# Weight decoding with a mask on VectorE and 16-bit words from ScalarE, and a first key chunk in two halves

## The chip, the core and the metric

The kernel runs on one core of a Trainium2 chip. The metric is the device time of one execution in microseconds; three runs of the kernel before took 966.6, 967.17 and 967.68 us, median 967.17. In the text PE is TensorE, DVE VectorE, ACT ScalarE, POOL GpSimd, and SP SyncE, whose queue issues most DMAs.

## The reference

Attention by random features, then a layer norm and a two-layer MLP with a residual. With q, k, v of 8 batches x 8 heads x 576 rows x 64, 128 features, d_model 512 and 2048 hidden units:

```python
def phi(x):
    proj = np.einsum('bhsd,md->bhsm', x, omega)
    sq = np.sum(x * x, axis=-1, keepdims=True) / 2.0
    h = proj - sq
    h = h - np.max(h, axis=-1, keepdims=True)
    return np.exp(h) / np.sqrt(m)
q_p, k_p = (phi(q_s), phi(k_s))
kv = np.einsum('bhsm,bhsd->bhmd', k_p, v)
z = np.sum(k_p, axis=2)
num = np.einsum('bhsm,bhmd->bhsd', q_p, kv)
den = np.einsum('bhsm,bhm->bhs', q_p, z)[..., None] + 1e-06
...
xn = (x - mu) / np.sqrt(var + 1e-06) * g_ln
ch = np.maximum(xn @ w_ch1, 0.0) @ w_ch2
return (x + ch).astype(np.float32)
```

Everything is float32 at the interface; the weights `w_ch1` and `w_ch2` arrive as float64 and are passed to the chip as pairs of 32-bit words.

## The kernel before

The 4608 rows (8 batches x 576) are cut into 36 chunks of 128 rows (`NC`), four chunks to a token tile of 512 (`T`), nine tiles (`NT`). The hidden layer is cut into 16 blocks of 128 (`NF`), called f below; `f` of `mm1` makes one block of 128 hidden units for a whole tile, `f` of `mm2` adds that block's share to the four output banks.

**Attention.** `gen_k` (lines 600 to 635) treats one key chunk: load, product with omega on PE into a pair of PSUM banks (L621, 16 matmuls), maximum on DVE (L624), eight exponentials on ACT (L630). `gen_sums` (L637) multiplies the result with v (L665) and copies the sum to `kv`. `gen_q` (L746) treats a query chunk: load, product (L767, or L784/L785 from tile 2 on), copy to SBUF, maximum over partitions on POOL (L796), subtraction on DVE (L801), exponential on ACT (L804). One chunk of the first tile, number 3, takes its maximum over PE instead (`gen_q_pe`). `gen_x` (L827) multiplies both (L850), divides (L857 to L861) and hands the rows to `gen_xnT` (L923), which normalises (L934/L936) and transposes them, the first tile through PE (L979, L983, L985), the others through a transposing DMA (`gen_flip`, L947 to L970).

**Weights.** `gen_w` (L501 to L557) loads one weight tile, `[128, 512]` float64 as two 32-bit words `r[:, :, 0]` (low) and `r[:, :, 1]` (high), and makes of it two float32r tiles, a leading part and a rest. The sign bit and the top three bits of the low word are put together with the scaled high word shifted by three. There are two ways. If the planner gives the first step to ACT, the low word is scaled there (L515) and DVE joins it with the sign bit (L517); if to DVE, DVE masks the sign (L523) and shifts and joins the low word (L527). Both then scale the high word on ACT (L360) or DVE (L362) and join all on DVE (L531); then come the factor g for some of them (L539), the leading part and the rest (L549/L555). There are 32 tiles, all made while the first token tile is in the MLP or before.

**MLP.** `mm1` (L1009 to L1011) and `mm2` (L1050 to L1052) each take three float32r matmuls in place of one full-precision one: 24 per hidden block, 12 each. `relu` (L1023 on ACT, L1025 on DVE) stands between them.

**The order.** All work is written as generators that `yield` their next need: an engine and an estimated duration, a tile, a bank, an event. The class `Plan` is a list scheduler that runs while the program is built: it keeps a clock for each engine, takes the work that can start first and, among equals, the lowest rank, and so writes each engine's fixed instruction order. `rank` is given at `plan.add`; a table `SHIFT` adds an offset to the ranks of named generators, for instance `('gen_x', 1): -42` for chunk 1 (L115, L1144). A token tile is worth 32 ranks, one hidden block two. A part that may run on ACT or DVE says so by `either(a, d)` with a duration for each.

Attention work that needs banks while the MLP runs is a *visit* (L420): it is let in between two MLP blocks in the bank pair 0 and 1. With two visits waiting, the MLP's own pair 2 and 3 is lent as well and both go in one interruption (`serve`, L189). Before the MLP starts there are three bank pairs for visits (`pairs_now`, L427), and small matmuls on a tile `spin` (`gen_warm`, L1083) fill PE's idle time.

Of the kernel before, what the change touches and what calls it, by code (L numbers as in the profile page):

```python
# [15 lines left out]
U32 = mybir.dt.uint32  # L16
U16 = mybir.dt.uint16
AF = mybir.ActivationFunctionType
# [5 lines left out]
P = 128  # L24
# [284 lines left out]
def favor_ffn(ctx, tc, kT, kTr, vF, vR, qT, qD, omT, gT, w1, w2, out):  # L309
# [21 lines left out]
    def f32(ap):  # L331
        return ap.bitcast(F32)
# [7 lines left out]
    def dve2(n):  # L340
        return "run", {DVE: 0.07 + 0.00104 * n}, "two"

    def either(a, d):
        return "run", {ACT: a, DVE: d}, "two"
# [156 lines left out]
    def gen_w(n, f):  # L501
# [8 lines left out]
        wt = yield "get", n_big  # L510
        eng = yield either(0.58, 0.34)
        t = tile_of(wt, [P, DM], U32)
        sign = 0x80000000
        if eng == ACT:
            nc.scalar.activation(out=t, in_=r[:, :, 0], func=AF.Copy, scale=2.0**-29 * 7.49 / 8)  # L515
            yield dve2(DM)
            nc.vector.scalar_tensor_tensor(  # L517
                out=r[:, :, 0], in0=r[:, :, 1], scalar=sign, in1=t, op0=ALU.bitwise_and, op1=ALU.bitwise_or
            )
            eng = yield either(0.58, 0.34)  # L520
            scaled(eng, f32(r[:, :, 1]), f32(r[:, :, 1]), 2.0**-112)
        else:
            nc.vector.tensor_scalar(out=t, in0=r[:, :, 1], scalar1=sign, scalar2=None, op0=ALU.bitwise_and)  # L523
            eng = yield either(0.58, 0.34)
            scaled(eng, f32(r[:, :, 1]), f32(r[:, :, 1]), 2.0**-112)
            yield dve2(DM)
            nc.vector.scalar_tensor_tensor(  # L527
                out=r[:, :, 0], in0=r[:, :, 0], scalar=29, in1=t, op0=ALU.logical_shift_right, op1=ALU.bitwise_or
            )
        yield dve2(DM)  # L530
        nc.vector.scalar_tensor_tensor(  # L531
            out=t, in0=r[:, :, 1], scalar=3, in1=r[:, :, 0], op0=ALU.logical_shift_left, op1=ALU.bitwise_or
# [67 lines left out]
    def gen_k(b, c, kraw, early, owners, t_v, n_kp, last):  # L600
# [4 lines left out]
        nc.sync.dma_start(kraw, kT[b, c] if c < NFULL else kTr[b // 2])  # L605
# [9 lines left out]

        t_b = yield from visit("row", 0.95)
# [18 lines left out]
        done(("kp", b, c))  # L635

# [109 lines left out]
    def gen_q(c):  # L746
# [3 lines left out]
        if c < QF:  # L750
            qraw = tile_of(t_q, [P, 4 * P])
            yield dma(P * 4 * P)
            if c == 0:
                nc.scalar.dma_start(qraw, qT[c].rearrange("p a b -> p (a b)"))
                nc.scalar.preload_act_table_set("natural_log_exp_and_others")
            else:
                nc.sync.dma_start(qraw, qT[c].rearrange("p a b -> p (a b)"))
# [446 lines left out]
```

## Time and profile before

| | us |
|---|---|
| median of three runs | 967.17 |
| the profiled execution | 966.85 |
| its span, first to last instruction | 965.0 |
| first matmul of the MLP (L1009) starts | 33.94 |
| busy: PE, DVE, ACT, POOL | 956.5, 446.1, 412.4, 118.3 |

The page gives each engine's busy time over the span; the windows give it by stage; the timeline lists instructions by start, length, engine, line, tiles written and read, and in brackets an idle time of the engine ahead of it with what ended it. `ACTq` and `SPq` rows are DMA issues. Rows of groups end with the total busy time, the mean in ns, and the idle time before them. A matmul's length in the rows is more than its distance to the next, since matmuls overlap in the array; distances between starts tell what one costs.

### The profile page before, as it was taken

To read this page: it belongs to the slowest core of one execution; us is meant where nothing else is said; L and a number is where in the kernel's file an instruction comes from. 1 tells how busy PE (TensorE), PEld (TensorE's weight loads), DVE (VectorE), ACT (ScalarE), POOL (GpSimd) and SP (SyncE) were. 2 spreads that over 40 slices of the span, in tenths; PEclk is the share of its full clock that TensorE was granted. 3 is DMA by queue.
4 is the path that set the end of the run, shared out by engine and by line. 5 is a ranking of instruction groups with operands and counts; after the bars stand their busy time and mean duration, and the time that the engine had idled before them with its cause. 6 is when DMAs were issued, how large, how long until landed. Compare 5 with 4: busy or idle time off the path is not lost.

```text
span 965.0 us, 15968 instructions
## 1 busy us (share of the span) xinstructions
PE 956.5 (99%) x6732; PEld 786.3 (81%) x6732; DVE 446.1 (46%) x779; ACT 412.4 (43%) x759; POOL 118.3 (12%) x47
## 2 busy tenths in 40 slices
PE   9999999999999999999999999999999999999998
PEld 6877788888888888888878888888888888888886
DVE  7999976434435445335635346561542131113112
ACT  7898855444245454345355435450332121011010
POOL 5003103104001120020303013320110000000000
PEclk9999999999999999999999999999999999999999
DMA  8765461352143324115233223240212030002001
GB/s 299 240 242 198 165 186 67 89 143 66 66 100 110 122 77 138 50 45 175 59 107 103 74 96 91 88 153 1 87 45 77 1 99 1 1 1 87 1 1 44
DMA packets 70584, 91.45 MB, mean 95 GB/s; under 512 B 38000, under 2 KB 38384, under 8 KB 70512
## 3 DMA queue, kind: packets, MB, share of 16 engines
q1 hardware_dynamic: 70368, 90.17, 29.2%
q8 instruction: 53, 0.87, 0.4%
q10 hardware_dynamic: 144, 0.26, 0.1%
q14 instruction: 19, 0.16, 0.1%
HBM read 63.15 MB, written 18.87 MB: 85 GB/s over the span
## 4 chain that ended last, share of the span: by engine, by line
PE 91%; DVE 3%; ACT 3%; DMA 2%; issue 1%; DVEq 0%; SPq 0%; ACTq 0%
PE b L1050 13%; PE b L1009 13%; PE b L1011 13%; PE b L1010 13%; PE b L1052 13%; PE b L1051 13%; PE b L665 4%; PE b L850 3%; PE b L621 3%; PE b L785 1%; PE b L784 1%; DMA wide<-wide 1%; DMA quad<-qD 1%; PE b L767 1%; DVE w L517 0%
## 5 line engine op out<-in xcount | busy, mean ns | idle before, releaser
L1025 DVE SCALAR_TENSOR_TENSOR hid<-b,hid 128x512 fp32r<-128x512 f32 x144 | 99.2, 690 | 340.4 <-ACT hid L1023 339.9
L1050 PE MATMUL b<-w,hid 128*128 128x512 f32 x577 | 228.9, 397 | 0.0
L1009 PE MATMUL b<-xnT,w 128*128 128x512 f32 (+1 forms) x584 | 227.3, 389 | 1.4 <-ACT kp L630 1.4
L1052 PE MATMUL b<-w,hid 128*128 128x512 f32 x577 | 225.2, 390 | 0.6 <-DVE hid L1025 0.5
L1011 PE MATMUL b<-xnT,w 128*128 128x512 f32 (+1 forms) x584 | 225.7, 386 | 0.0
L1010 PE MATMUL b<-xnT,w 128*128 128x512 f32 (+1 forms) x584 | 225.6, 386 | 0.0
L1051 PE MATMUL b<-w,hid 128*128 128x512 f32 x577 | 224.8, 390 | 0.0
L1023 ACT ACTIVATE hid<-b 128x512 fp32r<-128x512 f32 x144 | 85.8, 596 | 294.2 <-PE b L1011 293.9
L796 POOL PARTITION_ALL_REDUCE quad<-quad x34 | 112.1, 3321 | 596.9 <-ACT quad L354 423.9
L1009 PEld LDWEIGHTS b<-xnT,w 128*128 128x128 f32 x584 | 109.7, 188 | 27.1 <-ACT kp L630 2.5
L1052 PEld LDWEIGHTS b<-w,hid 128*128 128x128 f32 x577 | 108.3, 188 | 25.4 <-DVE hid L1025 2.5
L1050 PEld LDWEIGHTS b<-w,hid 128*128 128x128 f32 x577 | 108.3, 188 | 24.6
L1011 PEld LDWEIGHTS b<-xnT,w 128*128 128x128 f32 x584 | 109.7, 188 | 22.4
L1010 PEld LDWEIGHTS b<-xnT,w 128*128 128x128 f32 x584 | 109.7, 188 | 21.7
L1051 PEld LDWEIGHTS b<-w,hid 128*128 128x128 f32 x577 | 108.4, 188 | 21.4
L630 ACT ACTIVATE kp<-b,mb 128x128 f32<-128x128 f32 x264 | 71.9, 393 | 37.3 <-DVE mb L624 36.6
L934 ACT ACTIVATE wide<-x,st 128x512 f32<-128x512 f32 x29 | 20.9, 722 | 80.5 <-DVE x L861 69.6
L624 DVE TENSOR_REDUCE mb<-b 128x8 f32<-128x1024 f32 x36 | 42.9, 1218 | 26.4 <-PE b L621 26.2
L801 DVE TENSOR_TENSOR quad<-quad,quad 128x1024 f32<-128x1024 f32 x34 | 51.3, 1512 | 8.1 <-POOL quad L796 7.9
L779 DVE TENSOR_TENSOR quad<-quad,quad 64x1024 fp32r<-64x1024 f32 x28 | 37.6, 1342 | 27.3 <-ACT quad L777 27.1
L804 ACT ACTIVATE quad<-quad 128x1024 f32<-128x1024 f32 x35 | 37.6, 1089 | 28.7 <-DVE quad L801 28.6
L354 ACT COPY wide<-wide 128x1024 uint16<-128x1024 uint16 x26 | 35.0, 1356 | 33.4 <-DMA wide<-wide 33.3
(94 smaller groups left out, 761.4 us busy)
## 6 DMA issues: line engine op xcount, KB each, us to landing
w<-w SPq DMA_DIRECT2D x32, 512.0 KB, 7.0
quad<-qD SPq DMA_DIRECT2D x28, 512.0 KB, 4.1
away<-x SPq DMA_DIRECT2D x36, 256.0 KB, 2.8
x<-away SPq DMA_DIRECT2D x36, 256.0 KB, 3.5
out<-x SPq DMA_DIRECT2D x35, 256.0 KB, 2.0
v<-vF SPq DMA_DIRECT2D x28, 260.0 KB, 3.1
wide<-kT SPq DMA_DIRECT2D x28, 256.0 KB, 3.5
wide<-qT SPq DMA_DIRECT2D x7, 256.0 KB, 4.8
```

What stands on the lines that cost most here:

```text
L624: nc.vector.tensor_reduce(out=mb.rearrange("p (s a) -> p s a", s=2), in_=pk, axis=AX.X, op=ALU.max, negate=True)
L630: nc.scalar.activation(out=kp[:, j], in_=pk[:, s, j % 4], func=AF.Exp, scale=1.0, bias=mb[:, j : j + 1])
L796: nc.gpsimd.partition_all_reduce(mx.rearrange("p a b -> p (a b)"), qc.rearrange("p a b -> p (a b)"), P, bass_isa.ReduceOp.max)
L801: nc.vector.tensor_tensor(out=qc, in0=qc, in1=mx, op=ALU.subtract)
L1009: nc.tensor.matmul(ph[:, ts], w[:, 0, cs], xnT[:, 0, k, ts], start=k + i0 == 0, stop=False)
L1010: nc.tensor.matmul(ph[:, ts], w[:, 1, cs], xnT[:, 0, k, ts], start=False, stop=False)
L1011: nc.tensor.matmul(ph[:, ts], w[:, 0, cs], xnT[:, 1, k, ts], start=False, stop=k == NK - 1 and i1 == TC)
L1023: nc.scalar.activation(out=hl[:, 0], in_=ph, func=AF.Relu)
L1025: nc.vector.scalar_tensor_tensor(out=hl[:, 1], in0=ph, scalar=0.0, in1=f32(hl[:, 0]), op0=ALU.max, op1=ALU.subtract)
L1050: nc.tensor.matmul(accs[i][:, c], hl[:, 0, cs], w[:, 0, c], start=(f == 0), stop=False)
L1051: nc.tensor.matmul(accs[i][:, c], hl[:, 0, cs], w[:, 1, c], start=False, stop=False)
L1052: nc.tensor.matmul(accs[i][:, c], hl[:, 1, cs], w[:, 0, c], start=False, stop=f == NF - 1 and c == parts[-1])
```

## The change

The two ways of `gen_w` become one: the mask of the sign on DVE into a 32-bit tile `t`, then the low word, scaled on ACT and written as 16-bit into the lower half of each word of `t`; then the high word is scaled as before and one DVE pass joins it with `t`. The pass of L517 or L527 is gone.

The first key chunk (batch 0, chunk 0) is loaded by ScalarE's queue instead of SP's, with the table load behind it; the first query chunk, which had that place, is loaded by SP's queue. Its products, maximum and exponentials go in two halves of two head pairs each, through the new `gen_k_half`; both banks are freed when both halves are done.

`SHIFT` has 19 entries instead of 18, nearly all of them others.

```diff
         wt = yield "get", n_big
+        t = tile_of(wt, [P, DM], U32)
+        yield "run", {DVE: 0.34}, "two"
+        nc.vector.tensor_scalar(out=t, in0=r[:, :, 1], scalar1=0x80000000, scalar2=None, op0=ALU.bitwise_and)
+        yield us(ACT, 0.58)
+        low = t.bitcast(U16).rearrange("p (a b) -> p a b", b=2)[:, :, 0]
+        nc.scalar.activation(out=low, in_=r[:, :, 0], func=AF.Copy, scale=2.0**-29 * 7.49 / 8)
         eng = yield either(0.58, 0.34)
-        t = tile_of(wt, [P, DM], U32)
-        sign = 0x80000000
-        if eng == ACT:
...
-        else:
...
+        scaled(eng, f32(r[:, :, 1]), f32(r[:, :, 1]), 2.0**-112)
         yield dve2(DM)
         nc.vector.scalar_tensor_tensor(
-            out=t, in0=r[:, :, 1], scalar=3, in1=r[:, :, 0], op0=ALU.logical_shift_left, op1=ALU.bitwise_or
+            out=t, in0=r[:, :, 1], scalar=3, in1=t, op0=ALU.logical_shift_left, op1=ALU.bitwise_or
         )
...
-        nc.sync.dma_start(kraw, kT[b, c] if c < NFULL else kTr[b // 2])
+        if last:
+            nc.sync.dma_start(kraw, kT[b, c] if c < NFULL else kTr[b // 2])
+        else:
+            nc.scalar.dma_start(kraw, kT[b, c])
+            nc.scalar.preload_act_table_set("natural_log_exp_and_others")
...
+        if not last:
+            t_b = yield "pair", pairs_now()
+            pk = two(t_b).rearrange("p s (a b) -> p s a b", b=M)
+            left_k = [0, 1]
+            for i in range(2):
+                yield "run", {PE: 0.5}, 0.03
+                for p in range(2 * i, 2 * i + 2):
+                    for h in range(2):
+                        a = slice(h * D, (h + 1) * D)
+                        nc.tensor.matmul(pk[:, h, p], kraw[a, p], om[a], start=True, stop=True)
+                plan.add(rank, gen_k_half(b, c, i, pk, mb, kp, left_k, t_b, t_mb))
+            free(*early)
+            return
...
+    def gen_k_half(b, c, i, pk, mb, kp, left_k, t_b, t_mb):
+        cols = slice(2 * i, 2 * i + 2)
+        yield dve(4 * M)
+        nc.vector.tensor_reduce(
+            out=mb.rearrange("p (s a) -> p s a", s=2)[:, :, cols], in_=pk[:, :, cols], axis=AX.X, op=ALU.max, negate=True
+        )
+        yield us(ACT, 1.0)
+        for s in range(2):
+            for p in range(cols.start, cols.stop):
+                j = slot(2 * p + s)
+                nc.scalar.activation(
+                    out=kp[:, j], in_=pk[:, s, p], func=AF.Exp, scale=1.0, bias=mb[:, j : j + 1]
+                )
+        left_k.remove(i)
+        if not left_k:
+            free(*t_b)
+            free(t_mb)
+            done(("kp", b, c))
...
-            if c == 0:
-                nc.scalar.dma_start(qraw, qT[c].rearrange("p a b -> p (a b)"))
-                nc.scalar.preload_act_table_set("natural_log_exp_and_others")
-            else:
-                nc.sync.dma_start(qraw, qT[c].rearrange("p a b -> p (a b)"))
+            nc.sync.dma_start(qraw, qT[c].rearrange("p a b -> p (a b)"))
...
-SHIFT = {('gen_back', 3): 28, ('gen_k', 0, 1): 2, ('gen_k', 1, 1): -10, ('gen_q', 4): 50, ('gen_sums', 3, 0): 3, ('gen_v', 0, 4): 14, ('gen_v', 1, 0): 6, ('gen_v', 1, 1): 22, ('gen_var', 2): -15, ('gen_var', 3): -11, ('gen_w', 1, 0): 6, ('gen_w', 1, 2): 8, ('gen_w', 2, 0): 13, ('gen_w', 2, 15): -10, ('gen_w', 2, 3): -11, ('gen_x', 1): -42, ('gen_x', 5): -17, ('gen_x', 6): 11}
+SHIFT = {('gen_k', 0, 4): 8, ('gen_k', 2, 0): -9, ('gen_k', 5, 1): -27, ('gen_q', 2): -3, ('gen_q', 22): 34, ('gen_q', 7): 6, ('gen_sums', 2, 2): 2, ('gen_sums', 3, 0): 15, ('gen_v', 0, 0): 9, ('gen_v', 0, 3): 4, ('gen_v', 0, 4): 7, ('gen_v', 7, 0): -12, ('gen_w', 1, 7): -1, ('gen_w', 1, 8): 1, ('gen_w', 2, 1): -4, ('gen_x', 13): 45, ('gen_x', 4): 18, ('gen_x', 5): 21, ('gen_x', 6): -28}
```

More of the change, by code (lines that the diff above doesn't have):

```diff
@@ L510, in gen_w @@
         wt = yield "get", n_big
-        eng = yield either(0.58, 0.34)
-        t = tile_of(wt, [P, DM], U32)
-        sign = 0x80000000
-        if eng == ACT:
[L515 to L521, printed above, removed]
-        else:
[L523 to L529, printed above, removed]
+        t = tile_of(wt, [P, DM], U32)
[4 more added lines that the diff above has]
+        nc.scalar.activation(out=low, in_=r[:, :, 0], func=AF.Copy, scale=2.0**-29 * 7.49 / 8)
+        eng = yield either(0.58, 0.34)
+        scaled(eng, f32(r[:, :, 1]), f32(r[:, :, 1]), 2.0**-112)
         yield dve2(DM)
         nc.vector.scalar_tensor_tensor(
-            out=t, in0=r[:, :, 1], scalar=3, in1=r[:, :, 0], op0=ALU.logical_shift_left, op1=ALU.bitwise_or
+            out=t, in0=r[:, :, 1], scalar=3, in1=t, op0=ALU.logical_shift_left, op1=ALU.bitwise_or
         )
```

## The prediction

> **What bounds the kernel now.** I read the page first (engine shares, slices), then the windows by stage, then the timeline of each engine around the point at which the MLP starts, then the waits.
>
> ```profile
> span 965.0 us, 15968 instructions
> PE 956.5 (99%) x6732; PEld 786.3 (81%) x6732; DVE 446.1 (46%) x779; ACT 412.4 (43%) x759; POOL 118.3 (12%) x47
> 4.50:22.80 18.30, 17.96 (x274) 13.31 (x276) 15.14 (x23) 15.20 (x46) 9.78 (x4) 1.00 0.92 346
> 22.80:34.00 11.20, 10.87 (x232) 9.69 (x228) 10.92 (x30) 9.18 (x17) 0.00 (x0) 1.00 0.37 126
> 34.00:122.00 88.00, 87.85 (x627) 69.06 (x626) 86.02 (x152) 78.41 (x159) 13.31 (x4) 1.00 0.59 215
> ...
> 33.94 0.36 PE L1009 MATMUL b<-xnT,w 128*128 128x256 f32 x1
> ```
>
> The window rows give the length, then busy time of PE, weight loads, DVE, ACT, POOL, then the granted clock. The first MLP matmul starts at 33.94 (L1009). Before it PE's busy share is padded by the spin matmuls of `gen_warm`, so PE is no bound there: DVE is busy 15.14 + 10.92 = 26.06 of 29.5 us, ACT 15.20 + 9.18 = 24.38. After it the bound is PE: 87.85 of 88.00 us, at clock 1.00. In that stretch DVE is busy 86.02 of 88 too, yet PE waits for it nowhere by more than the 0.15 us that are missing. So the end moves one for one with the start of the MLP, with PE idle time after it, and with the switches between MLP and the attention's visits; DVE time saved after 34 us is worth nothing by itself.
>
> The profiled execution took 966.85 us for the 965.0 of the span, 1.85 lie around it; the median of the three runs, 967.17, is 0.32 above it. I sum against 966.85 and add 0.32 at the end.
>
> **Part 1, the first key chunk.** Its load goes from SP's queue to ScalarE's, where the first query chunk's was, and product, maximum and exponentials go in two halves.
>
> ```profile
> 0.73 0.39 ACTq L754 DMA_DIRECT2D wide<-qT  x1
> 1.20 0.43 SPq L605 DMA_DIRECT2D w<-kT  x1
> 1.20 3.21 DMA w<-kT
> 3.95 0.23 DVE L480 TENSOR_SCALAR om<-hid 128x128 f32<-128x128 f32 x1 [2.83 <-DMA hid<-omT]
> 4.54 1.51 PE L621 MATMUL b<-om,w 64*128 64x128 f32 x16 [0.23 <-DMA w<-kT]
> 6.09 1.22 DVE L624 TENSOR_REDUCE mb<-b 128x8 f32<-128x1024 f32 x1 [0.87 <-PE b L621]
> 6.95 1.01 ACT L354 COPY quad<-b 128x1024 f32<-128x1024 f32 x1 [4.51 <-PE b L767]
> 8.06 6.43 POOL L796 PARTITION_ALL_REDUCE quad<-quad  x2 [4.34 <-ACT quad L354]
> 16.54 4.36 ACT L630 ACTIVATE w<-b,mb 128x128 f32<-128x128 f32 x16
> ```
>
> The chunk was issued at 1.20 and landed 3.21 later, at 4.41; PE began 0.13 after that. Issued at 0.73 with the same flight it lands at 3.94, and what comes last is then `om`, ready at 3.95 + 0.23 = 4.18: PE begins at 4.31, 0.23 earlier. Half the products take 1.51/2 = 0.76, to 5.07. Half the reduce costs between 1.22/2 = 0.61 and the 0.69 of a 512-element DVE pass (rows of part 2): 0.65, to 5.7 and, with the gap of 0.04 that stands between L621's end and L624, about 5.8. ACT's first real work then starts at 5.8 in place of 6.95: 1.1 us earlier. It matters because from there ACT is the dense engine: 15.20 us of the stage, and the last exponentials of batch 0's five chunks end at 16.54 + 4.36 = 20.90. The extra reduce (2 x 0.65 - 1.22 = 0.1 on DVE) lies in DVE's first wait.
>
> The Trainium skill (Trainium Kernel Development and Optimization, Key Constraints) says that queues of several engines share the same DMA engines and that issuing from several saves only issue time. The two issue rows agree, 0.73 against 1.20; by it alone the move would be worth at most 0.47, and the trace allows only 0.23 of this.
>
> The query chunk pays: on SP's queue it takes the slot at 1.20 and lands at about 4.4, runs on PE behind both halves (5.8 to 6.9), and its copy, with ACT in exponentials, goes to DVE (1.21 us by the copy below), so POOL starts at 8.1 to 8.2 where it was 8.06. The other loads stand behind one 256 KB issue before and after; the value load of this chunk, now nine ranks later, frees SP a slot for the next keys. The price of the query chunk is 0.1 us on a chain (POOL) that does not end last. So part 1 is worth -1.1, between +0.1 (the query chain holds the stage) and -1.1.
>
> ```profile
> 8.31 1.21 DVE L356 COPY quad<-b 128x1024 f32<-128x1024 f32 x1 [0.44 <-PE b L767]
> 22.23 1.15 PE L665 MATMUL b<-w,w 128*64 128x65 f32 x32
> 23.43 0.59 ACT L354 COPY kv<-b 128x520 f32<-128x520 f32 x1
> 24.40 1.15 PE L850 MATMUL b<-kv,quad 128*64 128x65 f32 x32
> 32.52 0.68 DVE L531 SCALAR_TENSOR_TENSOR wide<-w 128x512 uint32<-128x512 uint32 x1
> 33.12 0.69 DVE L985 TENSOR_TENSOR xnT<-b,xnT 128x512 fp32r<-128x512 f32 x1
> ```
>
> The way from there to the MLP: the exponentials at 20.90 feed the last sum of batch 0 (22.23), its copy (23.43), the first numerators (24.40), then normalising and transposing, until L985 at 33.12 + 0.69 = 33.81 lets PE start at 33.94. A weight step (L531 at 32.52) stands right ahead of that L985.
>
> **Part 2, the weights.** In 30 of 32 tiles the scheduler chose ACT for the low word (L515), in two DVE (L523, L527).
>
> ```profile
> L531 DVE SCALAR_TENSOR_TENSOR wide<-w 128x512 uint32<-128x512 uint32 x32 | 21.0, 681 | 0.0
> L515 ACT ACTIVATE wide<-w 128x512 uint32<-128x512 uint32 x30 | 20.3, 690 | 1.9 <-DVE w L555 1.2 <-DVE w L549 0.6
> L517 DVE SCALAR_TENSOR_TENSOR w<-w,wide 128x512 uint32<-128x512 uint32 x30 | 19.9, 681 | 0.0
> L523 DVE TENSOR_SCALAR wide<-w 128x512 uint32<-128x512 uint32 x2 | 0.8, 424 | 0.0
> L527 DVE SCALAR_TENSOR_TENSOR w<-w,wide 128x512 uint32<-128x512 uint32 x2 | 1.3, 690 | 0.0
> ```
>
> Now every tile has the mask (L523's kind, 0.424) and the low word on ACT, and L531 alone remains. For the 30: 0.681 goes, 0.424 comes, -0.257 each, -7.7 us of DVE; for the two: -0.69 each, -1.4 of DVE and one ACT pass more each. The 16-bit write with a stride is in no row; the nearest is the same read of 512 words with a 32-bit write, 0.690; I take 0.69, and 1.04, a whole ACT pass of 1024 elements, as the upper end.
>
> Both tiles of the second kind were worked before the MLP began, as was the mask of one or two of the first kind: DVE has 2 x 0.69 + 0.257 = 1.6 us less there, ACT 2 x 0.69 = 1.4 more. ACT has room for that, just not everywhere:
>
> ```profile
> 24.52 1.03 ACT L741 ACTIVATE quad<-b 128x1024 f32<-128x1024 f32 x1 [0.50 <-PE b L733]
> 26.47 0.62 ACT L354 CAST w<-wide 128x512 fp32r<-128x512 f32 x1 [0.41 <-DVE wide L539]
> 29.10 0.69 ACT L360 ACTIVATE w<-w 128x512 f32<-128x512 f32 x1 [0.93 <-DVE w L517]
> ```
>
> These idle stretches are 0.50 + 0.41 + 0.93 = 1.84 us and cover the 1.4. Of DVE's 1.6 most sat before 24.4, where the end of the stage hangs on the exponentials; only passes that stand among the four L861 and L985 count. I take -0.4, one weight pass less ahead of an L985, between the ends of -1.6 (all of it) and +1.4 (ACT's passes delay the copies at 23.43 or the later ones). Together: MLP start 33.94 - 1.1 - 0.4 = 32.4.
>
> After that, DVE's other 7.5 us go from a stretch in which PE does not wait: 0. The cover is the backlog of attention work that DVE then does sooner. The change adds one wait per tile: ACT's low word waits for DVE's mask, and behind it on ACT stand whatever exponentials and MLP relus the planner put there; a mask that is late by its own 0.424 holds a relu by as much, and PE then waits only if its other block of 24 matmuls has run out. SP's order of the first weight loads changes too. Both at nothing: all of PE's waits between 34 and 122 are 0.15 us now.
>
> **Part 3, the ranks.** They reorder DVE's, ACT's and PE's visits all through. What a visit costs alone or paired:
>
> ```profile
> 44.72 0.39 PE L1011 MATMUL b<-xnT,w 128*128 128x512 f32 x1
> 45.04 1.16 PE L621 MATMUL b<-om,wide 64*128 64x128 f32 x16
> 46.47 0.39 PE L1010 MATMUL b<-xnT,w 128*128 128x512 f32 x1
> ...
> 102.44 1.13 PE L767 MATMUL b<-wide,om 64*128 64x512 f32 x4
> ...
> 185.05 0.39 PE L1052 MATMUL b<-w,hid 128*128 128x512 f32 x1
> 185.37 2.06 PE L621 MATMUL b<-om,wide 64*128 64x128 f32 x32
> 187.69 0.39 PE L1051 MATMUL b<-w,hid 128*128 128x512 f32 x1
> ...
> 148.00 0.39 PE L1052 MATMUL b<-w,hid 128*128 128x512 f32 x1
> 148.23 0.39 PE L1009 MATMUL b<-xnT,w 128*128 128x512 f32 x1
> PE b L1009 <- ACT kp L630: 1.4, 2, 1.1
> ```
>
> Undisturbed MLP matmuls start 0.23 us apart (148.00, 148.23). A lone key visit takes 46.47 - 44.72 - 2 x 0.23 = 1.29 out of the MLP, two in one 187.69 - 185.05 - 0.46 = 2.18: a pair saves 2 x 1.29 - 2.18 = 0.40. Between 34 and 122 six lone key or query visits stand in the timeline, 45.04 the first, 102.44 the last: three pairs at most, 1.2 us. Keys that come sooner off a lighter DVE make one pair more likely than none: -0.4. The last row, from the waits, gives the cause, total, count and longest: PE's two waits for a lent bank, 1.4 us. They could go or double; I take them as they are. Ends: -1.2 - 1.4 = -2.6, and the rival below.
>
> **Sum.** -1.1 - 0.4 + 0 - 0.4 = -1.9: 966.85 - 1.9 = 964.95, and with 0.32 965.3 for the median.
>
> **Rivals.** First, the start gains little: ACT's two added passes fall between 20.9 and 24.0, ahead of the kv copy, rather than into its idle time. Then +1.4 stands against the -1.1 and -0.8: 966.85 - 0.5 = 966.35, in the median 966.7. For it: ACT is the dense engine there; against: the weights rank behind the copies. The Trainium skill (ScalarE: Activation LUTs, Rules for kernel authors) advises VectorE rather than ScalarE for plain multiplications, which speaks against moving the low word. The rows of this case bear that out only in part: L515 takes 0.690 on ACT and L527 0.690 on DVE.
>
> Second, the new order also takes away the lent-bank waits and pairs all the lone visits: a further -1.4 - 0.8 = -2.2, 963.1. For it: each of these depends on two visits being ready together; against: nothing in the diff touches banks.
>
> Third, slower, at the change to the second token tile:
>
> ```profile
> 146.63 0.69 DVE L968 TENSOR_TENSOR xnT<-wide,xnT 128x512 fp32r<-128x512 f32 x1 [0.70 <-ACT xnT L354]
> ```
>
> The tile's last piece was ready at 146.63 + 0.69 = 147.32, PE took it up at 148.23 (row above): 0.91 to spare, and with an MLP 1.5 earlier the piece is needed 0.6 before it was there. The ranks of chunks 4 and 5 go back by 18 and 38. If one of these visits slips by a block of 24 matmuls (24 x 0.23 = 5.5), PE stands 5.5 + 0.6 = 6.1 us: 964.95 + 6.1 + 0.32 = 971.4. It decides from a slip of -0.6 on, that is, already if nothing comes earlier. Against it: DVE is relieved of 9.1 us up to there, and DVE was the engine that held this chain.
>
> **How the numbers follow.** About 0.2% (1.93 us, so 965.24 and 969.10) is what a measurement can tell from no change. Forecast 0.43, own range 964.2 to 966.4, so cut nearly in half by the lower line (0.21 faster, 0.22 same). Start gains little 0.21, same. Waits and pairs gone too 0.24, faster. Second tile late 0.12, slower. Faster 0.45, same 0.43, slower 0.12. The range reaches down past the second rival to 962.6 and up to 968.4, which leaves out the third and a little below.
>
> **What would show it.** First exponential near 5.8 (right) or after 6.5 (part 1 wrong); last exponentials of batch 0 near 19.8; first L1009 near 32.4; a 16-bit low word near 0.69 on ACT and 32 masks near 0.42; between the MLP's start and end the same PE time less 0.4. If the MLP starts at 33.5 or later, or an idle stretch over 1 us stands ahead of an L1009 at a tile's start, the forecast is wrong.

## The result, and the profile after

The kernel after takes 972.41 us (median of seven runs, 970.06 to 974.42), the kernel before, run beside it, 966.6 us (964.45 to 967.68): ratio 1.0055, 95% interval 1.0041 to 1.0070. The change costs 5.8 us where the prediction had -1.9. The profiled execution of after took 971.31 us, 4.46 more than that of before; the traces below account for these 4.46. The rest goes with the wider spread of after, which the last section takes up.

The page of after, first the span, then busy time and count of each engine:

```profile
span 969.3 us, 15968 instructions
PE 953.9 (98%) x6715; PEld 785.4 (81%) x6715; DVE 452.1 (47%) x799; ACT 403.6 (42%) x741; POOL 118.7 (12%) x47
```

PE's recorded time is slightly less (with 17 matmuls fewer on record) and the span is 4.3 longer: PE stands. The windows of after, in the prediction's columns, the second and third cut at after's own start of the MLP:

```profile
4.50:22.80 18.30, 14.94 (x235) 11.77 (x237) 13.97 (x19) 13.50 (x43) 9.78 (x4) 1.00 0.86 319
22.80:34.77 11.97, 11.22 (x252) 9.63 (x248) 11.52 (x33) 8.83 (x14) 0.00 (x0) 1.00 0.38 121
34.77:122.00 87.23, 85.52 (x596) 67.97 (x595) 83.28 (x162) 73.02 (x149) 12.68 (x4) 1.00 0.61 220
122.00:152.28 30.28, 28.50 (x285) 23.45 (x283) 20.44 (x44) 18.83 (x28) 0.58 (x1) 1.00 0.57 158
```

In the first row DVE and ACT are both less busy than before (13.97 for 15.14, 13.50 for 15.20): the start is not denser, it waits. In the third and fourth PE lacks 1.71 and 1.78 us. Comparing PE's timelines, after lies behind before by 0.83 us at the first MLP matmul, 2.21 at the 25th (the "first whole block" of the expectations below: the first matmul behind two groups of 12, between which after has the last transposes), 4.05 at the start of the second token tile and 4.75 at the last matmul. Three places, then: the start, the change to the second tile, and a smaller one later.

**The start.** The timeline of after, all engines, in order of time (start, length, engine, line, operation, tiles; in brackets the idle time ahead and what ended it):

```profile
4.28 1.75 PE L618 MATMUL b<-om,w 64*128 64x128 f32 x16
6.08 0.69 DVE L646 TENSOR_REDUCE mb<-b 128x4 f32<-128x512 f32 x1 [1.86 <-PE b L618]
6.80 1.14 ACT L653 ACTIVATE kp<-b,mb 128x128 f32<-128x128 f32 x4 [4.36 <-DVE mb L646]
7.97 0.69 DVE L646 TENSOR_REDUCE mb<-b 128x4 f32<-128x512 f32 x1 [1.21 <-ACT kp L653]
8.66 1.22 DVE L356 COPY quad<-b 128x1024 f32<-128x1024 f32 x1
9.98 6.43 POOL L817 PARTITION_ALL_REDUCE quad<-quad  x2 [6.27 <-DVE quad L356]
16.46 3.30 POOL L817 PARTITION_ALL_REDUCE w<-quad  x1
16.91 3.73 DVE L822 TENSOR_TENSOR quad<-quad,quad 128x1024 f32<-128x1024 f32 x2
20.57 1.21 DVE L741 TENSOR_REDUCE w<-b 128x8 f32<-128x1024 f32 x1
21.83 0.33 PE L746 MATMUL b<-ident,w 128*128 128x128 f32 x1 [1.52 <-DVE w L586]
34.77 0.36 PE L1030 MATMUL b<-xnT,w 128*128 128x256 f32 x1
37.69 0.39 PE L1031 MATMUL b<-xnT,w 128*128 128x256 f32 x1 [0.48 <-DVE w L544]
39.11 0.28 PE L1030 MATMUL b<-xnT,w 128*128 128x256 f32 x1
```

The halves are none. The first maximum waits for all 16 products, and the second (7.97) for the first half's exponentials, because each half lies in both banks of the pair and the program keeps engines apart bank by bank (two experiments below test this). The first query chunk's copy stands behind that second maximum on DVE, so POOL begins at 9.98. Read down from there: POOL's third maximum, the subtractions L822 that overlap it, the maximum L741 of query chunk 3, and its transpose on PE (L746), with the sums of batch 0 queued behind. No bracket there names POOL: the first of the two subtractions lasts 2.60 us in place of 1.22, because POOL is at its maximum meanwhile (last section). The same steps in the trace of before:

```profile
14.54 3.30 POOL L796 PARTITION_ALL_REDUCE w<-quad  x1
16.96 1.16 PE L714 MATMUL b<-om,wide 64*128 64x128 f32 x16
18.22 1.23 DVE L716 TENSOR_REDUCE w<-b 128x8 f32<-128x1024 f32 x1 [0.59 <-POOL w L796]
19.50 0.33 PE L721 MATMUL b<-ident,w 128*128 128x128 f32 x1
36.90 0.28 PE L1009 MATMUL b<-xnT,w 128*128 128x256 f32 x1
```

16.46 against 14.54 is 1.92 later, 20.57 against 18.22 2.35, 21.83 against 19.50 2.33, 39.11 against 36.90 2.21: the delay of POOL goes through to the MLP. Before, POOL had started at 8.06. The first maximum on DVE starts at the same time in both (6.08 and 6.09), so the whole 1.92 arises between it and POOL.

In before this chain was not the last one. The bracket of L716 names POOL, but POOL's maximum had ended at 17.84, 0.38 us earlier, and elsewhere in this trace a subtraction that waits for POOL starts 0.03 us behind it. The products that L716 reads (L714) ended at 18.12, 0.10 before it. The subtraction on DVE ahead of L716 had ended 0.59 before L716 began, and behind the transpose at 19.50 PE still ran spin matmuls up to the sums at 20.08. So POOL had some tenths of a microsecond to spare, and 1.92 is more than that.

**The second token tile.** ACT, SP, DVE and PE of after around its start:

```profile
139.52 0.43 SPq L793 DMA_DIRECT2D quad<-qD  x1
145.08 1.05 ACT L798 CAST quad<-quad 128x1024 fp32r<-128x1024 f32 x1 [1.63 <-DMA quad<-qD]
146.03 0.59 ACT L1044 ACTIVATE hid<-b 128x512 fp32r<-128x512 f32 x1
146.65 0.69 DVE L1046 SCALAR_TENSOR_TENSOR hid<-b,hid 128x512 fp32r<-128x512 f32 x1 [2.36 <-ACT hid L1044]
147.40 2.06 PE L627 MATMUL b<-om,wide 64*128 64x128 f32 x32 [1.78 <-DVE hid L1046]
```

The load of query chunk 10 was issued at 139.52 and landed only at about 145.07; ACT, in order, stood 1.63 us at the cast that needs it, with a relu of the MLP behind; DVE's part of the relu waited for ACT and PE for DVE. PE's bracket names DVE, the engine at fault is ACT, and the cause is a DMA.

**Later.** Of the last 0.7 us the largest piece is one wait:

```profile
540.15 1.31 ACT L354 COPY wide<-wide 128x1024 uint16<-128x1024 uint16 x1
541.34 4.22 ACT L636 ACTIVATE kp<-b,mb 128x128 f32<-128x128 f32 x16
542.51 0.50 PE L1030 MATMUL b<-xnT,w 128*128 128x512 f32 x1 [1.80 <-ACT kp L636]
```

A key visit sits in the MLP's own lent banks, and its exponentials stand behind a copy of 1.31 us that is not urgent. Before's longest wait of this kind was 1.1.

**The weights** (groups of after; total us, mean ns):

```profile
L516 ACT ACTIVATE wide<-w 128x512 uint16<-128x512 uint32 x32 | 24.6, 804 | 5.5 <-DVE wide L513 5.4
L520 DVE SCALAR_TENSOR_TENSOR wide<-w,wide 128x512 uint32<-128x512 uint32 x32 | 22.0, 702 | 2.6 <-ACT w L360 1.7 <-ACT wide L516 0.9
L513 DVE TENSOR_SCALAR wide<-w 128x512 uint32<-128x512 uint32 x32 | 12.6, 419 | 0.0
```

All 32 tiles have the mask, the 16-bit low word and one join, and the passes L517 and L527 are gone. The 16-bit write costs 0.804 us, not 0.69.

### The profile page after: what moved, and what is told of

Same layout as the page of the kernel before. It is cut to its first block, busy times and chain, and to the rows that moved or that the text cites. A ratio compares the mean times of both kernels' runs of the same rounds, so it can differ in the third digit from the quotient of the medians.

```text
span 969.3 us, 15968 instructions
## 1 busy us (share of the span) xinstructions
PE 953.9 (98%) x6715; PEld 785.4 (81%) x6715; DVE 452.1 (47%) x799; ACT 403.6 (42%) x741; POOL 118.7 (12%) x47
## 4 chain that ended last, share of the span: by engine, by line
PE 84%; DVE 6%; ACT 5%; DMA 2%; issue 1%; POOL 0%; SPq 0%; DVEq 0%; ACTq 0%; POOLq 0%
PE b L1071 12%; PE b L1030 12%; PE b L1073 12%; PE b L1072 12%; PE b L1032 12%; PE b L1031 12%; PE b L690 4%; PE b L871 3%; PE b L627 3%; DMA quad<-qD 2%; PE b L805 1%; PE b L806 1%; ACT kp L636 1%; DVE wide L520 1%; DVE w L544 1%
## 5 line engine op out<-in xcount | busy, mean ns | idle before, releaser
L636 ACT ACTIVATE kp<-b,mb 128x128 f32<-128x128 f32 x256 | 69.6, 392 | 39.1 <-DVE mb L630 39.0
L822 DVE TENSOR_TENSOR quad<-quad,quad 128x1024 f32<-128x1024 f32 x34 | 55.8, 1647 | 11.1 <-POOL quad L817 11.0
L800 DVE TENSOR_TENSOR quad<-quad,quad 64x1024 fp32r<-64x1024 f32 x28 | 35.0, 1253 | 20.1 <-ACT quad L798 19.9
```

The lines of the kernel that those rows point to most:

```text
L636: nc.scalar.activation(out=kp[:, j], in_=pk[:, s, j % 4], func=AF.Exp, scale=1.0, bias=mb[:, j : j + 1])
L822: nc.vector.tensor_tensor(out=qc, in0=qc, in1=mx, op=ALU.subtract)
```

## The experiments

### Each part alone

Four kernels: before with the new `gen_w` only; with the new `SHIFT` only; with the first key chunk's new load and halves only; and after with the old `SHIFT`, so with both other parts.

The first has only the hunk of `gen_w` of the diff above, the third only those of the first key chunk and the query load; the other two exchange one line:

```diff
 (ranks alone, on before)
-SHIFT = {('gen_back', 3): 28, ('gen_k', 0, 1): 2, ('gen_k', 1, 1): -10, ('gen_q', 4): 50, ...}
+SHIFT = {('gen_k', 0, 4): 8, ('gen_k', 2, 0): -9, ('gen_k', 5, 1): -27, ('gen_q', 2): -3, ...}
 (old ranks, on after)
-SHIFT = {('gen_k', 0, 4): 8, ('gen_k', 2, 0): -9, ('gen_k', 5, 1): -27, ('gen_q', 2): -3, ...}
+SHIFT = {('gen_back', 3): 28, ('gen_k', 0, 1): 2, ('gen_k', 1, 1): -10, ('gen_q', 4): 50, ...}
```

> The kernel before with the new weight decoding alone: old first key chunk, old ranks. Theory (the order that the scheduler writes is fitted to one set of durations, so any part alone costs through waits in new places): slower than before by 2 to 15 us. Rival (one part carries the loss, and it is the other): within 2 us of before, or faster by up to 2 as VectorE is relieved.

> The kernel before with the new table of ranks alone. Theory: slower than before by 5 to 20 us, as the ranks belong to the other two parts. Rival (the new ranks are harmless by themselves): within 2 us of before.

> The kernel before with the first key chunk in two parts and the two loads exchanged, old weights, old ranks. Theory: MLP start 0.5 to 2 us later than 33.94 through the query copy, and some us of waits later: slower by 2 to 15 us. Rival (this part does what it says): MLP start 0.5 to 1.1 sooner, time 0.5 to 1.1 below before.

> The changed kernel with the table of ranks of the kernel before. Theory (the new ranks are no loss by themselves; they are fitted to a start that does not happen): MLP start within 1.5 us of 34.77, other waits in other places, time 968 to 974. Rival (the new ranks are what makes it slower): the waits near 147 and 540 go, time 966 to 968.

Measured: weights only 980.01 us (ratio 1.0136, 1.0118 to 1.0154), ranks only 976.9 (1.0103, 1.0081 to 1.0124), key chunk only 989.96 (1.0245, 1.022 to 1.0271), weights and key chunk with the old ranks 983.06 (1.0169, 1.0156 to 1.0182). Every part costs 10 to 23 us alone; all three together cost 5.8. So the parts can't be priced one by one and added: each changes the durations or ranks from which the planner writes the order of all five engines, and ranks that suit one set of durations need not suit another (argued from how the planner works; the runs show only that the parts don't add up). That holds for the new ranks too: added to the weights and the key chunk they bring 983.06 down to 972.41, alone they cost 10. Where the loss sits differs from one to the next. With the weights alone the MLP starts only 0.51 later (34.45), but PE's timeline counts 93 interruptions of the MLP by visits in place of 77; with the ranks alone the MLP itself starts at 39.54. With the key chunk alone one wait of PE has

```profile
154.93 0.80 PE L816 MATMUL b<-quad,om_hi 128*128 128x512 f32 x1 [3.44 <-ACT kp L647]
```

From here on the experiments keep the order that the planner wrote for after, on every engine, but for what is named.

### Halves that use their own columns

```diff
-        nc.vector.tensor_reduce(out=mb.rearrange(...)[:, :, cols], in_=pk[:, :, cols], ...)
+        for s in range(2):
+            m = slice(4 * s + 2 * i, 4 * s + 2 * i + 2)
+            nc.vector.tensor_reduce(out=mb[:, m], in_=pk[:, s, cols], ...)
```

> The changed kernel with the same order on every engine, but each half's maximum taken by two reduces of one bank each, into two adjacent columns, so that no range of one half lies across the other. Theory (the halves are halves in name only: the first maximum waits for all 16 products, the second for the first half's exponentials, and the first query copy queues behind it on VectorE): first maximum before 5.6 instead of 6.08, first query copy on VectorE about 0.8 to 1.6 us before 8.66, first maximum over partitions on GpSimd 0.8 to 1.6 before 9.98, MLP start 33.3 to 34.2 instead of 34.77, time 0.6 to 1.5 us below the changed kernel. Rival (the start is held by the low words on ScalarE and the reordered weights): MLP start 34.6 to 34.9, same time.

Measured: 972.68 us (1.0062, 1.005 to 1.0074), no change. Its timeline on DVE:

```profile
6.17 0.76 DVE L648 TENSOR_REDUCE mb<-b 128x2 f32<-128x256 f32 x2 [1.98 <-PE b L618]
7.29 0.94 DVE L648 TENSOR_REDUCE mb<-b 128x2 f32<-128x256 f32 x2 [0.36 <-ACT kp L653]
```

The waits still stand, first for the products, then for the other half's exponentials, though the second is shorter (0.36 in place of 1.21), and POOL starts 3.37 behind the first maximum in place of 3.90. What is shared is the bank and not the columns. The Trainium skill (PSUM — Partial Sum Buffer, PSUM bank collisions raise a hardware error) asks for exactly this, to guard PSUM by bank and quadrant and not by address; by it halves that share banks and partitions can't overlap, and the rows agree.

### The second maximum off the banks

```diff
-        nc.vector.tensor_reduce(out=mb.rearrange(...)[:, :, cols], in_=pk[:, :, cols], ...)
+        if i == 0:
+            for s in range(2):
+                nc.vector.tensor_reduce(out=mb[:, 4*s : 4*s+2], in_=pk[:, s, cols], ...)
+        else:
+            for s in range(2):
+                nc.vector.tensor_reduce(out=mb[:, 4*s+2 : 4*s+4], in_=kraw[:, 2*s : 2*s+2], ...)
```

> The changed kernel with the same order, but the second half's maximum is taken from the raw keys in SBUF, as many elements, not from the PSUM banks (so the exponentials of that half are offset by another number than the reference's). Theory (the second maximum waits for the first half's exponentials because both read the same two banks, and the first query copy stands behind it): the wait of 1.2 us ahead of it goes, query copy near 7.6, first maximum over partitions near 8.9 (9.98 in the changed kernel's profile), MLP start 33.2 to 34.2, time 0.5 to 1.5 us below the changed kernel. Rival (the first query copy waits for other things, and the start is given by later ones): MLP start as in the changed kernel, 34 to 35, and its time.

Measured: 971.55 us (1.0047, 1.0032 to 1.0062), 0.9 less than after with overlapping intervals. DVE's timeline:

```profile
6.10 0.73 DVE L651 TENSOR_REDUCE mb<-w 128x2 f32<-128x256 f32 x2
7.61 0.17 DVE L485 TENSOR_SCALAR g_sb<-g_sb 128x4 f32<-128x4 f32 x1 [0.66 <-DMA g_sb<-gT]
7.68 1.22 DVE L356 COPY quad<-b 128x1024 f32<-128x1024 f32 x1
```

Without the shared banks the second maximum waits for nothing, and the copy comes 1.0 sooner (7.68 for 8.66). Of that, 0.66 is already there at the first maximum (5.42 for 6.08), which this edit does not move; its own part is 0.32. The copy could have come at 6.9: the next instruction on DVE waits 0.66 for the load of g.

### One maximum for both halves

```diff
-        nc.vector.tensor_reduce(out=mb.rearrange(...)[:, :, cols], in_=pk[:, :, cols], ...)
+        if i == 0:
+            nc.vector.tensor_reduce(out=mb.rearrange(...), in_=pk, ...)
```

> The changed kernel with one maximum over the whole first key chunk (the pass of 8 columns, 1.22 us) where its first half's maximum stood, and none for the second half; products, exponentials, loads and every engine's order stay. Theory 'POOL chain' (the query copy stands on VectorE behind the second half's maximum, so POOL's three maxima, the subtraction behind them and then the sums of batch 0 on PE come later by the same time): the maximum runs from 6.1 to 7.3, the copy from about 7.4, POOL starts at about 8.7 in place of 9.98, PE's first whole MLP block 1.2 to 1.4 us sooner than 39.11, and the time is about 971.1. Rival 'ScalarE' (the low words ahead of the kv copies hold the start): POOL sooner, the first block not, 972.4.

Measured: 970.55 us (1.0046, 1.0029 to 1.0064). DVE, POOL and PE of this kernel:

```profile
5.65 1.23 DVE L647 TENSOR_REDUCE mb<-b 128x8 f32<-128x1024 f32 x1 [1.55 <-PE b L618]
8.82 6.43 POOL L818 PARTITION_ALL_REDUCE quad<-quad  x2 [5.10 <-DVE quad L356]
37.95 0.28 PE L1031 MATMUL b<-xnT,w 128*128 128x256 f32 x1
```

POOL comes 1.16 sooner than in after and the 25th MLP matmul 1.16 sooner (37.95 for 39.11). The same holds over all the kernels with after's order of the start; the times are from their timelines:

```
kernel                first max  next query    POOL's      25th MLP  POOL to
                      on DVE     products, PE  first max   matmul    25th
after                   6.08        9.38         9.98       39.11    29.13
columns of their own    6.17        8.42         9.54       38.66    29.12
load sooner             5.29        8.60         9.20       38.33    29.13
word of 32 bits         6.36        9.67        10.27       39.39    29.12
second max off banks    5.42        7.60         9.00       37.86    28.86
one max                 5.65        8.62         8.82       37.95    29.13
one max, load           5.63        8.61         8.41       37.53    29.12
one max, load, copy     6.43        9.40         9.12       38.24    29.12
```

The distance from POOL to the 25th matmul stays within 0.01 in seven of eight kernels while the start wanders over 1.9 us (with columns of their own, two differences of 0.2 cancel: L741 comes 0.21 sooner behind POOL, a wait for a weight is 0.19 longer). A rival is the way through the banks: the exponentials, then the next query products on PE, then what stands behind these; the profile's own chain of after goes this way. The table speaks against it: after and the last kernel have these products at the same time (9.38, 9.40), and the 25th matmul 0.87 apart, as POOL (0.86). So in this order POOL's chain sets the start of the MLP.

The table also shows how far one profile can be trusted. Three kernels that are the same up to 20 us (after, load sooner, word of 32 bits) start POOL at 9.98, 9.20 and 10.27, so single start times scatter by half a microsecond or more either way. The scatter is there at the first maximum already, and POOL follows it by 3.90 to 3.91 in all three. It comes from PE: the trace has PE's clock full from 5.54, 3.87 and 6.31 us on in these profiles, and pairs of key products start 0.21 us apart ahead of that and 0.11 apart behind it; the first maximum waits for all of them. So of the 1.16 that one maximum gains here, 0.43 stands ahead of its edit, and 0.73 is its own (POOL 3.17 behind the first maximum in place of 3.90).

### The low word at 32 bits

```diff
-        low = t.bitcast(U16).rearrange("p (a b) -> p a b", b=2)[:, :, 0]
-        nc.scalar.activation(out=low, in_=r[:, :, 0], ...)
+        nc.scalar.activation(out=t, in_=r[:, :, 0], ...)
```

> The changed kernel with the low word written as 32-bit over the whole of the mask's tile (the sign is lost, so the weights come out without it), same order. Theory (the 16-bit write with a stride costs ScalarE more than the 32-bit one): mean of the low word from 804 ns to about 690, ScalarE 3.5 us less busy, time 0 to 1 us below the changed kernel, as only what stands ahead of the MLP or of a relu counts. Rival (the mean is longer because of what runs beside it): mean stays near 800 and the time too.

Measured: 973.38 us (1.0073, 1.006 to 1.0085). The group of the low word in this kernel:

```profile
L515 ACT ACTIVATE wide<-w 128x512 uint32<-128x512 uint32 x32 | 21.1, 687 | 5.6 <-DVE wide L513 5.4 <-issue 0.2
```

The write of 32 bits takes 687 ns in place of 804, 3.5 us less of ACT's busy time in all, and the time is no better (the intervals overlap). So the dearer pass of the new weights isn't what made the kernel slower. The 25th MLP matmul follows POOL by 29.12, and the waits at the second tile and in the lent banks stand in this profile as in after (2.01 and 1.80).

### The load of query chunk 10, sooner

```diff
-            yield dma(P * 8 * P)
+            if c != 10:
+                yield dma(P * 8 * P)
             nc.sync.dma_start(qraw..., qD[c - QF]...)
+            if c == 10:
+                yield dma(P * 8 * P)
```

> The changed kernel with one instruction moved: the load of query chunk 10 stands eight places sooner on SyncE's queue; all else in the same order. Theory (at the end of the first token tile ScalarE stands at the cast of this chunk, the last relu of the tile stands behind it, and TensorE waits 1.78 us for the bank): the wait of 1.8 us ahead of the key visit near 147 falls under 0.5, the second tile starts 1.2 to 1.8 us sooner, time 1 to 1.8 us below the changed kernel. Rival (the second tile waits for its transposed rows anyway): the wait only moves to the first matmul of the second tile, time within 0.5 us of the changed kernel.

Measured: 970.32 us (1.0036, 1.0024 to 1.0048), 2.1 less than after, with intervals that overlap by a little; 1.0 to 1.8 had been expected. SP and PE:

```profile
131.10 0.33 SPq L794 DMA_DIRECT2D quad<-qD  x1
145.48 2.06 PE L627 MATMUL b<-om,wide 64*128 64x128 f32 x32 [0.63 <-DVE hid L1049]
```

Issued at 131.10, the load no longer holds ACT; PE waits 0.63 in place of 1.78 and starts the second tile at 150.36 in place of 152.28: the lag there falls from 4.05 to 2.13 us. Of this 0.78 is the start of this profile, which came sooner by itself (39.11 against 38.33), and 1.14 the shorter wait.

### Both repairs

```diff
+        if i == 0:
+            nc.vector.tensor_reduce(out=mb.rearrange(...), in_=pk, ...)
...
+            if c == 10:
+                yield dma(P * 8 * P)
```

> The one maximum, and the load of query chunk 10 issued 8 places sooner on SP's queue as in the run with the sooner load. Theory 'separate places': both gains add, since the first lies before the MLP and the second at the change to the second tile: 972.4 - 1.3 - 2.1 = about 969.0. Rival 'given back': an earlier start makes the second tile's last piece late again, and the sum is no better than the sooner load alone, 970.3.

Measured: 970.19 us (1.0032, 1.002 to 1.0043): better than after by 2.2, but no better than the load alone. The rows look like the rival "given back":

```profile
142.10 1.36 ACT L354 COPY wide<-wide 128x1024 uint16<-128x1024 uint16 x1 [2.52 <-DMA wide<-wide]
145.63 2.06 PE L627 MATMUL b<-om,wide 64*128 64x128 f32 x32 [1.56 <-DVE hid L1050]
```

The MLP runs 0.8 sooner than with the load alone, and now ACT stands 2.52 us one instruction ahead, at the transposing DMA of a piece of the next tile; PE waited 1.56. But that DMA was issued sooner here (136.15) than with the load alone (136.94) and landed at about the same time (ACT's copy at 142.10 and 141.94): it took 5.9 us in this profile and 5.0 there. In the next kernel, which has both repairs too, it took 4.7, and PE waits 0.69 at this place. So a slow transfer in one profile took the gain, and the medians of both kernels lie within each other's intervals. Whether the two gains add stays open.

### One copy off ScalarE

```diff
         eng = yield either(1.27, 1.13)
+        if (t, i) == (6, 0):
+            eng = DVE
         copy(eng, whole..., flipped...)
```

> As the run before it, and one copy of a transposed piece (tile 6, piece 0), which runs on ScalarE at 540.15 for 1.31 us ahead of sixteen exponentials of a visit in the lent banks, goes to VectorE between that visit's two maxima. Theory 'order on ScalarE': the exponentials start about 1.0 sooner, PE's wait of 1.80 at 542.5 shrinks to about 0.8, 968.0. Rival: the wait is moved to the copy's readers or to the next visit, and the time stays at 969.0.

Measured: 969.01 us (1.0020, 1.0010 to 1.0031), 1.2 below the kernel with both repairs, with intervals that overlap; 968.0 had been expected. DVE and PE:

```profile
538.36 0.73 DVE L356 COPY wide<-wide 128x1024 uint16<-128x1024 uint16 x1
539.67 0.50 PE L1036 MATMUL b<-xnT,w 128*128 128x512 f32 x1 [0.81 <-ACT kp L636]
```

The exponentials no longer stand behind the copy and PE's wait is 0.81 instead of 1.80, as expected.

### The copy ahead of the exponentials

```diff
-        copy(eng, qc, pq)
+        copy(ACT if c == 0 else eng, qc, pq)
+        while held:
+            pk, mb, kp, cols = held.pop(0)
+            for s in range(2):
+                for p in range(cols.start, cols.stop):
+                    j = slot(2 * p + s)
+                    nc.scalar.activation(out=kp[:, j], in_=pk[:, s, p], func=AF.Exp, ...)
```

`held` takes the two halves of `gen_k_half` in place of its own loop of exponentials.

> As the last run, and the first query chunk's copy goes to ScalarE ahead of the first key chunk's eight exponentials, where the kernel before has it; with it both of the first key chunk's novelties but its load are undone. Theory 'POOL chain': POOL starts at about 8.1 (8.41 to 9.12 in the three kernels with one maximum), PE's first whole MLP block comes 29.1 later, at about 37.2, though the first key chunk's exponentials now start at about 7.9 and not at 6.8; 968.3. Rival 'exponentials': ScalarE is the dense engine there, and exponentials that start 1.1 later hold the sums of batch 0: the first block at 38.2 or later, 969.0 to 970. Third: what the start gains is given back at the second tile, 969.0.

Measured: 969.64 us (1.0021, 1.0013 to 1.0030): no gain on 969.01, the intervals overlap. POOL, PE and PE again:

```profile
8.75 3.22 POOL L826 PARTITION_ALL_REDUCE quad<-quad  x1 [5.04 <-ACT quad L354]
10.27 2.50 PE L786 MATMUL b<-wide,om 64*128 64x512 f32 x8 [1.78 <-ACT kp L818]
16.48 3.22 POOL L826 PARTITION_ALL_REDUCE w<-quad  x1
39.04 0.28 PE L1041 MATMUL b<-xnT,w 128*128 128x256 f32 x1
```

The first maximum of POOL comes at 8.75, but the 25th matmul at 39.04, 30.3 later: the law above is broken. The exponentials, now second on ACT, hold the key chunk's banks, the next query products wait 1.78 us for these (10.27), and so POOL's third maximum is as late as in after (16.48 for 16.46). From that third maximum the distance is 22.56, against 22.65 in after: it is the link that counts. My theory was too short by one step, and the rival "exponentials" was right, by way of the banks. In after's order the query copy and the exponentials both have to come soon; that halves with banks of their own would have given both is argued, and no run here has them.

## Why the prediction was wrong

**Part 1, the first exponentials at 5.8 and a start 1.1 sooner: wrong.** They came at 6.80. The step that failed first is "Half the products take 1.51/2 = 0.76": half the products free nothing as long as both halves lie in the same two banks. PE did begin sooner, as forecast (4.28, 4.31 expected), but all 16 products were done no sooner (the next on PE start at 5.87, before at 5.88): pairs of them start 0.21 apart until PE's clock is full, at 5.54 us (5.31 in before), and 0.11 apart after that. So 1.51 us for 16 products is not a fixed size at this point. The rest of the gain went with it; in ACT's timeline the last exponentials of batch 0 end at 20.95 (20.90 before), and not near 19.8.

**"The price of the query chunk is 0.1 us on a chain (POOL) that does not end last": the costly error.** The price was 1.92. The step under it is "The extra reduce (2 x 0.65 - 1.22 = 0.1 on DVE) lies in DVE's first wait": the second half's reduce stood behind the first half's exponentials instead (1.21 of wait and 0.69 for itself), and the copy that POOL needs stood behind it on DVE. That the chain does not end last was true of before, but by some tenths of a microsecond only; with 1.92 more it ends last, through the stretched subtraction, DVE's L741 and PE's L746. I judged the chain by POOL's own idle time instead of following it to its last reader and asking how much it had to spare there. The 25th matmul moved by +2.21, the MLP's first by +0.83, where -1.5 was forecast. Of the 2.21, 1.93 arise between the first maximum and POOL and 0.29 behind POOL. One maximum in place of two gives 0.73 back.

**Part 2, the weights: right in its counts, off in one size, and worth nothing as said.** 32 masks at 0.419, joins at 0.702, low words at 0.804 instead of 0.69. The 32-bit word shows that this size decides nothing. DVE's busy time rose all the same (452.1 for 446.1) and ACT's fell (403.6 for 412.4), in the whole span. The planner shifted choosable passes to DVE (13 high words on L362 where there were 3, five query copies where there were three); I had held these choices fixed. And the subtractions L822 got longer beside POOL, 55.8 us in place of 51.3.

**Part 3, the ranks: one pair more, as taken.** Between the MLP's start and 122 us four lone key or query visits are left (the first at 55.90, the last at 117.07), before there were six. "I take them as they are", said of the waits for lent banks, failed: 1.80 us at 542.5, of which moving one copy recovers 1.0.

**The rivals.** The third had the side and the place, the change to the second tile, and nearly the number (971.4), for another reason. No visit slipped by a block; a load was issued late enough to hold ACT, the relu behind it and PE for 1.78 us, and the start was 2 us later, not 1.5 sooner. Given 0.12, it deserved more: the prediction itself showed only 0.91 us to spare there. The sign by which the forecast was to be known as wrong, an MLP that starts at 33.5 or later, came (34.77).

**What the sum becomes.** In the profiles: start +2.21, second tile +1.84 (4.05 - 2.21), later +0.70, and 4.75 at the last matmul; less what ends the span, 4.46 between the executions. Undone one after the other (one maximum, sooner load, one copy moved), the 5.8 us above before become 1.7 (969.01 against 967.26, the 19 runs of before on that chip): about 4.1 of 5.8. The three are shown together; each alone has an interval that overlaps its neighbour's. What stays, 1.7 us, is in that kernel's profile 1.34 at the 25th matmul and 0.6 more by the end. Of the 1.34, 0.34 stand at the first maximum (6.43 for 6.09), in the part that scatters with PE's clock, 0.72 lie between it and POOL, and 0.28 behind POOL. Among the first 24 matmuls stand four transposes (36.31 in after) and a wait of 0.48 for a weight; before has all its transposes ahead of the MLP and no wait there. What these cost by themselves was not tried, and the 0.6 at the end stays open. No version ran faster than before.

## What to carry to other kernels

Before giving two engines "halves" of a tile, see what the waits are kept by: halves that share banks are one piece with an extra wait, and what stands behind that wait pays. Price the transfer or copy that makes room for something else by following its chain to the last reader, through in-order neighbours on every engine, and not by how idle its own engine looks; write down how much the chain has to spare there, since a price beyond that goes through. Check a bracket against the end of the engine that it names (here 0.38 us off). Where a planner writes the order from estimated durations, a changed duration is a change of the whole order: its parts don't add up (here +10 to +23 us each, +5.8 together), and the waits that come are found in the trace, not in the diff.

## What was not expected of the hardware

**A wait of 1.8 us can halve PE's clock.** The kernel with words of 32 bits has the same 1.80 us wait as after (at 544.88), and after it PE's matmuls stand 0.43 us apart instead of 0.23 until 549.10. That costs about 1.6 us (eight matmuls at 0.20 more each). Its trace has the granted clock full from 6.31 on, half from 149.67 to 153.08 (behind the wait of 2.01 at the second tile) and from 545.62 to 549.03. Each stretch lasts 3.41 us, and they start 42 and 158 times 3.413 us after 6.31. All half-clock stretches between a profile's first full clock and its last matmul, in the 14 profiles, lie on such a grid. So the clock is decided window by window. Two windows and what follows each (PE's busy time is the first number behind the length, the granted clock the third from the end), first from this kernel, then from the one with columns of their own:

```profile
542.20:545.62 3.42, 1.62 (x7) 1.02 (x7) 1.58 (x2) 3.42 (x10) 0.00 (x0) 1.00 0.01 2
545.62:549.03 3.41, 3.41 (x9) 2.65 (x9) 0.00 (x0) 2.31 (x9) 0.00 (x0) 0.50 0.00 0
```

```profile
145.75:149.17 3.42, 1.88 (x32) 1.86 (x32) 2.59 (x4) 3.14 (x5) 0.00 (x0) 1.00 0.02 5
149.17:152.58 3.41, 3.41 (x18) 2.53 (x15) 3.35 (x5) 1.60 (x7) 0.00 (x0) 1.00 0.00 0
```

The first window holds the whole wait of 1.80, and the next one is at half clock. In the second kernel the wait is longer, 2.08 (until 147.29), but it begins in the window before and only 1.54 of it lie in this one: the clock stays full. After's own 1.80 is split as 0.72 and 1.08. Counted over all windows of the 14 profiles, from the first full clock to the last matmul, eight hold 1.80 us or more of PE's idle time (up to 2.92; once it is two waits of 1.08 and 0.75 that lie 0.5 apart), and half clock follows each; of the others, which hold up to 1.78, it follows one only, the window at half clock in which the longest wait (3.44, key chunk alone) ends. The eight lie in the profiles of the 32-bit words, the ranks alone, the weights alone, the key chunk alone and the old ranks. Before, whose longest wait in the MLP is 1.1, has none. After's two long waits (1.78 and 1.80) lie at the edge, and whether they cost a stretch in a run without a profile depends on where its windows fall; that is argued.

It fits the spread: of the six runs of the kernel with one maximum, four lie at 970.13 to 970.74 with a mean granted clock of 0.999 to 1.0, and two at 973.42 and 973.94 with 0.996 and 0.998. So part of the 1.1 us by which after's median lies above its profiled execution may be such stretches; of after's runs the three with 0.997 or 0.998 are at 972.41, 973.58 and 974.42 and the three with 0.999 at 970.06 to 971.79, but one of 972.82 has 1.0. The Trainium skill (TensorE: Matmul & The Clock Gate, Part 1: The HAM clock gate) has the clock decided in free-running windows of about 3.4 us; the grid agrees. The Trainium skill (TensorE: Matmul & The Clock Gate, Why this matters for your kernels) names idle gaps over about 3 us as what to avoid; here 1.80 us in one window were enough, and the measurement decides.

**DVE beside POOL.** The subtraction L822 lasts 1.22 us alone and up to 2.9 while POOL takes a maximum:

```profile
L822 DVE TENSOR_TENSOR quad<-quad,quad x34: 1208/1224/2921, 16.9 to 722.0; 128x1024 f32<-128x1024 f32 x34
```

(minimum, median and longest in ns). All ten of after's subtractions that are stretched in this way end 0.25 us before POOL's maximum does, however early they began. So it is in the start of four kernels, where the first one begins at 16.91 (after), 16.15 (one maximum), 16.93 (one copy off ScalarE) and 17.80 (copy first) and lasts 2.60, 2.20, 1.72 and 1.65. At 16.91 two of them take 3.73 us in place of 2.44, and L741 behind them starts 4.1 us after POOL's third maximum begins, in after as with one maximum (20.57 - 16.46; 19.40 - 15.30), though the subtractions began 0.76 apart. That is why POOL's chain sets the start even where no bracket names POOL. With the second maximum off the banks, the first subtraction began before POOL's third maximum (15.35, 15.48) and was not stretched; there the distance in the table is 28.86. The Trainium skill (GPSIMD Engine Reference, Specifications) says that POOL shares its SBUF interfaces with VectorE instructions that have two SBUF inputs, as L822 has; the rows agree.
